# Gated mixer and attention kernel: the change of stage between the first layer and the attention, with first phases among full products, the last gelu among the first exponentials, and the first k and q loaded during the last pass

## The chip, the cores and the metric

One NeuronCore of a Trainium2 chip runs the whole program. The time is device microseconds of that core for one execution; the median of several executions counts, and one further execution was taken by the hardware profiler. Engines are named as in the profile: PE is TensorE (PEld its weight loads), ACT is ScalarE, DVE is VectorE, POOL is GpSimd, SP is SyncE, which only issues DMAs.

## The reference

The input x has 2048 tokens of 512 channels. Two branches are mixed by a gate per token.

```python
g = _sigmoid((x * gate_w).sum(-1, keepdims=True))
a = _A_ref(x, A_wqkv, A_wo)                # attention: 32 heads of 16, softmax over 2048 keys, then wo
b = _B_ref(x, B_w1, B_b1, B_w2, B_b2)      # layernorm; over tokens: w1 (2048 to 1792), gelu, w2 (1792 to 2048)
return g * a + (1 - g) * b
```

All tensors are float32. The kernel writes a float32 operand as a high and a low part and multiplies hi x hi, hi x lo and lo x hi, so that one product of the reference is three matmuls.

## The kernel before

The program is one function, gated_mix, in four stages.

1. **Values, keys, queries** (to about 139 us in the profile). x is loaded, turned and split; v stays in SBUF. k and q of all heads are computed, split into parts and stored to DRAM (kp, qp). The shift of the exponent's argument is a further 16 rows per head: in q the bound, stored in qp; in k the constant -1.
2. **First layer** (L460 to L523, to 290.9 us). The 1792 rows of u are made in four passes over f0: three of 512 rows, the last of 256. A pass has 16 steps, one for each 128 tokens; the last one goes through the second half of the tokens first, then the first half. Each step needs one block of w1: `load_weight` has SP load it (w_raw, 4 buffers), `split_weight` casts it on ACT (w_hi, 3 buffers) and subtracts on POOL (w_lo). `weight()` loads and splits ahead: in the last three steps of the last pass the blocks split are already the first ones of w2. I call these **A, B, C, D**: A holds rows 0 to 3 (of 14 blocks of u) for the first tile of outputs, B 4 to 7, C 8 to 11, D 12 and 13. When a pass is over, `gelu` (L468) takes each of its banks through add (DVE), Square (ACT), scale and multiply (DVE), Tanh (ACT), a further multiply (DVE), a cast to u_hi (ACT) and a subtraction to u_lo (DVE). The gelus of one pass run beside the next one. Those of the last pass, numbers 12 and 13, have no next pass: the loop at L521 runs them after it.
3. **Attention with the second layer beside it** (L883 on, to about 1260 us). 32 groups (16 pairs of heads, two halves of the queries) have 8 phases each, of 8 score matmuls of 64 rows. In the other 64 rows of TensorE runs half of a matmul of the second layer: a product is done in two halves in two phases (`dense`, a list by pairs of phases; L1024). Behind a phase come the value matmuls of the phase before (`apply_v`, L861). ACT takes the exponentials of the scores (L926) out of a ring of seven banks, so the eighth score of a phase waits for a bank of its own phase. In some phases DVE computes one pair of exponentials instead. Ahead of the first phase the list `first` holds 28 full products of the second layer (128 rows each, L892); 14 x 3 = 42 products make one tile of outputs.
4. **The end**: output projections, gate, stores.

k and q of a pair of heads stand stacked in tiles ks (two buffers) and qs: `load_k` (L552) brings three blocks of 16 rows for each of two heads, 128 KB each, `load_q` (L557) four of 64 KB. The rows of -1 in the two k buffers are memset: the first on POOL (L541), the second on DVE (L1039) at the end of phase 0. The k buffers lie where the first layer's second half of h lay, so the first load of k can start when the last pass has left that half.

What sets the order: inside `tc.manual_schedule(...)` the instructions of the named engines keep the order of the code (all five engines in stage 3; ACT, DVE and POOL in the first and last pass of the first layer). Two such parts, and what stands outside, are merged by the framework's scheduler by priority. Each engine then works its own queue strictly in order. Every DMA here is issued by SP, whose queue is one more such queue; a DMA also waits there for the eighth before it.

Of the kernel before, what the change touches and what calls it, by code (L numbers as in the profile page):

```python
# [76 lines left out]
def gated_mix(ctx: ExitStack, tc: tile.TileContext, a_x, a_wqkv, a_wo, b_w1, b_b1, b_w2, b_b2, gate_w, out):  # L77
# [18 lines left out]
    qp_d = [dram.tile([3, P, S], F32, name=f"qp{b}") for b in range(ND)]  # L96
    most_d = dram.tile([P, ND], F32, name="most_d")
    kp_d = [dram.tile([2, P, S], F32, name=f"kp{b}") for b in range(ND)]

# [60 lines left out]
    def weight():  # L160
        load_weight()
        split_weight()
        return ready.pop(0)
# [24 lines left out]
    with tc.tile_pool(name="vp", bufs=1, side="right") as pool:  # L188
# [74 lines left out]
        with tc.manual_schedule():  # L263
# [64 lines left out]
            for t in range(2, NS):  # L328
                if t + 1 < TURNED:
                    turn(t + 1)  # L330
                if t + 2 < NS:
                    turn_blocks(t + 2)
                row_stats(t - 2)
                if t + 5 < NS:
                    load_blocks(t + 5)
                if t + 3 < NS:
                    load(t + 3)
                if t == 4:
                    turn_biases(bias_tiles)
                if t in (6, 9):  # L340
                    qk_w.append(load_wcols(qk_cols.pop(0)))
                if t in (9, 12):
                    qk_w.append(split_wcols(*qk_w.pop(0)))
                ps = bank()
                products(ps, v_pairs(t))
                v_out(t, ps)
# [119 lines left out]
    with tc.tile_pool(name="ln1", bufs=3, side="right") as ln, tc.tile_pool(name="gl", bufs=2, side="right") as gl:  # L466

        def gelu(ps, fb):  # L468

            u = gl.tile([P, D], F32, name="gu")  # L470
            s = gl.tile([P, D], F32, name="gs")
            hi, lo = u_hi[:, fb, :], u_lo[:, fb, :]
            nc.vector.tensor_scalar_add(u, ps, b1[:, fb : fb + 1])
            yield
            nc.scalar.activation(s, u, AF.Square)
            yield
            nc.vector.tensor_scalar(s, s, GELU_A, 1.0, ALU.mult, ALU.add)
            nc.vector.tensor_mul(s, s, u)
            yield
            nc.scalar.activation(s, s, AF.Tanh, scale=GELU_C)  # L480
# [13 lines left out]
        STEPS = 7  # L494
        gelus = []
        for f0, cs in order.items():
# [37 lines left out]

    def shift_rows(engine, t):
        for i in range(2):
            engine.memset(t[i * HALF + SHIFT[0] : i * HALF + SHIFT[0] + DH].bitcast(F32), -1.0)


    with tc.issue_after(subs[-1].ins):  # L540
        shift_rows(nc.gpsimd, k_bufs[0])  # L541


    def stack(dst, src, which, pair, cols, planes):
        b, r0 = divmod(pair * 2 * DH, P)
        for i in range(2):
            rows = slice(r0 + i * DH, r0 + (i + 1) * DH)
# [3 lines left out]

    def load_k(g):  # L552
        t = k_bufs[g % 2]
        stack(t, kp_d, 1, g % NP, slice(0, S), PAIRS)
        return t

    def load_q(g):  # L557
        half, pair = divmod(g, NP)
        t = stk.tile([P, QW], F32R, name="qs")
        stack(t, qp_d, 0, pair, slice(half * QW, (half + 1) * QW), [*PAIRS, SHIFT])  # L560
        return t

    def second_out(t, ps):
        bp = out_pool.tile([P, D], F32, name="row", bufs=3)
        nc.vector.tensor_scalar(bp, ps, b2x2[:, t : t + 1], omg[:, t : t + 1], ALU.add, ALU.mult)
        nc.sync.dma_start(bp_d[t], bp)

    acc_ctx.close()

# [182 lines left out]
    steps = second_layer(0)  # L752
    first, at = steps[:28], put(steps[28:], 0, [8, 6])
    for t in range(1, NS):
# [129 lines left out]
    with tc.manual_schedule(engines=engines):  # L884
        kt, qt = {0: load_k(0)}, {0: load_q(0)}
        late, fence = None, None

        for n, (step, *args) in enumerate(first):
            if n and n % 12 == 0:
                split_weight(nc.vector.tensor_copy, nc.vector.tensor_tensor)  # L890
            ps, a, b, start, stop, done = step(*args)
            nc.tensor.matmul(ps, a, b, start=start, stop=stop)  # L892
            if done:
                done()

# [80 lines left out]
        for grp in range(NG):  # L976
            at = [0, 0]
            for ph in range(2 * TWOS):
# [237 lines left out]
```

## Time and profile before

| | |
|---|---|
| median of 3 runs | 1272.56 us (1272.41 to 1272.59) |
| profiled execution | 1272.19 us |
| its span, first to last instruction | 1270.4 us |
| TensorE busy | 1261.4 us, 99% of the span |
| ScalarE, VectorE, GpSimd busy | 84%, 57%, 18% |
| granted TensorE clock | 0.999 |
| end of the first layer, first score, first value product | 290.9, 298.0, 303.5 us |

A matmul of 512 columns shows as 0.39 us, but the next one starts 0.23 us after it, since they are pipelined; what counts is the distance of the starts. In a timeline row stand start, duration, engine, line, operation, tiles and count, and in brackets how long the engine was idle before and what ended that. A row with a count xN covers N instructions that follow each other.

### The profile page before, as it was taken

The numbers are of one execution on the slowest core, as the hardware profiler recorded it, in microseconds if no ns is written. First come the engines' busy times: TensorE is split into PE (matmuls) and PEld (weight loads), VectorE is DVE, ScalarE is ACT, GpSimd is POOL, SyncE is SP. The second block draws the span as 40 slices with busy tenths as digits, with TensorE's granted clock in tenths as the row PEclk, the third lists the DMA queues.
The fourth block names the chain that finished last, engine by engine and source line by source line (L and its number), as shares of the span: only waits on it lengthen the run. The fifth ranks groups of instructions, "written<-read, shape, count | busy, mean of one in ns | idle before, by whom it ended". The sixth has DMA issues, their size and how long they took to land.

```text
span 1270.4 us, 33041 instructions
## 1 busy us (share of the span) xinstructions
PE 1261.4 (99%) x13230; PEld 797.6 (63%) x13230; DVE 725.9 (57%) x1329; ACT 1072.8 (84%) x1484; POOL 229.4 (18%) x447
## 2 busy tenths in 40 slices
PE   9999999999999999999999999999999999999997
PEld 7888888886555555555555555555555555555555
DVE  6775371537776776666634346676666662325425
ACT  4444343438999999999999999999999999999994
POOL 4510244453111111111110011111111111100000
PEclk9999999999999999999999999999999999999999
DMA  7787633327343343334555533333334345447721
GB/s 203 209 292 290 230 111 100 98 75 160 72 93 60 76 86 70 77 67 85 114 106 118 131 64 71 68 73 76 75 72 73 76 89 103 98 87 195 151 61 70
DMA packets 101554, 140.53 MB, mean 111 GB/s; under 512 B 17081, under 2 KB 62287, under 8 KB 98320
## 3 DMA queue, kind: packets, MB, share of 16 engines
q1 hardware_dynamic: 100816, 137.29, 46.0%
q8 instruction: 106, 1.74, 0.6%
q10 hardware_dynamic: 576, 1.05, 0.2%
q14 instruction: 56, 0.46, 0.1%
HBM read 102.25 MB, written 36.03 MB: 109 GB/s over the span
## 4 chain that ended last, share of the span: by engine, by line
PE 98%; DMA 1%; ACT 0%; DVE 0%; issue 0%; SPq 0%
PE s L861 38%; PE s L903 33%; PE acc L464 12%; PE acc L91 10%; PE dn L1024 4%; PE pa L1095 1%; PE acc L298 0%; DMA ks<-kp 0%; ACT pt L926 0%; PE acc L271 0%; DMA qs<-qp 0%; PE pa L1104 0%; PE acc L209 0%; DVE base L1117 0%; SPq L149 0%
## 5 line engine op out<-in xcount | busy, mean ns | idle before, releaser
L926 ACT ACTIVATE pt<-s 128x512 f32<-128x512 f32 (+1 forms) x1259 | 943.7, 961 | 10.1 <-PE s L903 4.9
L903 PE MATMUL s<-qs,ks 64*128 64x512 f32 x2048 | 494.0, 404 | 1.4 <-DMA qs<-qp 0.6
L861 PE MATMUL s<-pt,v 128*17 128x256 f32 x8024 | 482.6, 381 | 0.0
L903 PEld LDWEIGHTS s<-qs,ks 64*128 64x128 f32 x2048 | 325.2, 184 | 168.7 <-ACT pt L926 91.2
L881 DVE TENSOR_TENSOR ot<-s,ot 128x256 f32<-128x256 f32 (+2 forms) x427 | 190.4, 447 | 348.4 <-PE s L861 272.3
L861 PEld LDWEIGHTS s<-pt,v 128*17 128x17 f32 x8024 | 210.3, 97 | 232.5 <-ACT pt L926 85.0
L1024 PE MATMUL dn<-u_hi,w_hi 64*128 64x512 f32 x428 | 186.5, 436 | 0.0
L84 POOL TENSOR_TENSOR w_lo<-w_raw,w_hi 128x512 fp32r<-128x512 f32 (+1 forms) x126 | 148.7, 1182 | 169.4 <-ACT w_hi L83 109.7
L1024 PE MATMUL dn<-u_lo,w_hi 64*128 64x512 f32 x430 | 170.1, 395 | 0.0
L1024 PE MATMUL dn<-u_hi,w_lo 64*128 64x512 f32 x430 | 169.1, 393 | 0.0
L1028 POOL MEMSET token<- 1x1 f32 x256 | 26.4, 103 | 780.0 <-PE dn L1024 659.4
L948 DVE SCALAR_TENSOR_TENSOR row<-row,o_hi 128x512 f32<-128x512 f32 x168 | 116.6, 694 | 4.9
L83 ACT CAST w_hi<-w_raw 128x512 fp32r<-128x512 f32 (+1 forms) x67 | 37.9, 569 | 80.3 <-PE acc L464 59.9
L464 PE MATMUL acc<-h_hi,w_hi 128*128 128x512 f32 x224 | 87.1, 389 | 0.0
L464 PE MATMUL acc<-h_lo,w_hi 128*128 128x512 f32 x224 | 87.1, 389 | 0.0
L464 PE MATMUL acc<-h_hi,w_lo 128*128 128x512 f32 x224 | 87.1, 389 | 0.0
L1024 PEld LDWEIGHTS dn<-u_hi,w_lo 64*128 64x128 f32 x430 | 79.3, 184 | 1.3
L1024 PEld LDWEIGHTS dn<-u_lo,w_hi 64*128 64x128 f32 x430 | 79.4, 185 | 0.5
L1024 PEld LDWEIGHTS dn<-u_hi,w_hi 64*128 64x128 f32 x428 | 78.6, 184 | 1.1
L91 PE MATMUL acc<-xt_hi,wc_hi 128*128 128x512 f32 x128 | 49.8, 389 | 0.0
L91 PE MATMUL acc<-xt_lo,wc_hi 128*128 128x512 f32 x128 | 49.8, 389 | 0.0
L91 PE MATMUL acc<-xt_hi,wc_lo 128*128 128x512 f32 x128 | 49.8, 389 | 0.0
(148 smaller groups left out, 1163.6 us busy)
## 6 DMA issues: line engine op xcount, KB each, us to landing
w_raw<-in_B_w_dram SPq DMA_DIRECT2D x96, 256.0 KB
ks<-kp SPq DMA_DIRECT2D x192, 128.0 KB
qs<-qp SPq DMA_DIRECT2D x256, 64.0 KB
qp<-pc SPq DMA_DIRECT2D x16, 768.0 KB
x<-in_A_x_dram SPq DMA_DIRECT2D x32, 256.0 KB
kp<-pc SPq DMA_DIRECT2D x16, 512.0 KB
w_raw<-in_B_w_dram SPq DMA_DIRECT2D x32, 128.0 KB
bp<-row SPq DMA_DIRECT2D x16, 256.0 KB
```

Source lines behind the costliest of these rows:

```text
L83: copy(hi, src)
L84: return sub(lo, src, hi.bitcast(F32), ALU.subtract)
L91: nc.tensor.matmul(ps, a, b, start=start and n == 0, stop=stop and n == last)
L464: nc.tensor.matmul(p, a, b, start=first and k == 0, stop=last and k == 2)
L861: mm = nc.tensor.matmul(av[32 * j : 32 * j + VC, i * QC : (i + 1) * QC], v[:, c, g % NP * 2 + i, :], pt[:, h * QC : (h + 1) * QC], start=t ...
L881: reads(nc.vector.tensor_tensor(x, y, x, ALU.add), bank)
L903: mm = nc.tensor.matmul(banks[:, bank, :], kt[grp][rows, c * P : (c + 1) * P], qt[grp][rows, qb * NB : (qb + 1) * NB], start=True, stop=True,)
L926: act = nc.scalar.activation(dst, banks[:, at[0] : at[-1] + 1, :], AF.Exp, scale=SCALE)
L948: nc.vector.scalar_tensor_tensor(box[1], q or box[1], a, x, ALU.add, ALU.mult)
L1024: mm = nc.tensor.matmul(ps, a[half], b[half], start=first and not second, stop=last and bool(second))
L1028: fence = nc.gpsimd.memset(token, 0.0)
L1095: nc.tensor.matmul(pa[t], a, b, start=i == 0 and t not in LATE, stop=i == len(mms) - 1 and t in LATE)
```

## The change

- **Order of the second layer's first tile.** `first` has the products 0 to 15; the next 8 (16 to 23) go as halves beside the scores of phases 0 and 1; a new list `between` has products 24 to 35 as full ones, put behind the scores of phase 0 and ahead of those of phase 1; the last six go with phases 2 and 3 as before.
- **Gelus 12 and 13.** Their add is issued where the loop at L521 stood, the next four steps of both ahead of `first`, and the last two (cast and subtraction) after each of the first four scores of phase 0. Since their buffers are gone by then, they take tiles of the later stage (row, ot).
- **First k and q.** `load_k` and `load_q` can load one head alone. The four loads of the first pair are issued with the priority of given steps of the last pass (the list `marks` holds the priority at each step).
- **Rows of -1.** A DRAM tensor minus_d is filled once, in the value stage (POOL memset and one store by SP at tile 5); load_k copies it into each k buffer the first time. The memsets of POOL and DVE go.
- **Splits.** Block D is split on DVE at the end of phase 0; the two splits among `first` go.

```diff
+    minus_d = dram.tile([DH, S], F32, name="minus_d")
...
+                if t == 5:
+                    minus = pool.tile([P, DH * S // P], F32, name="minus")
+                    nc.gpsimd.memset(minus, -1.0)
+                    nc.sync.dma_start(minus_d.rearrange("r (a c) -> (r a) c", a=P // DH), minus)
...
-        def gelu(ps, fb):
+        def gelu(ps, fb, places=None):
...
+            u, s = places() if places else (gl.tile([P, D], F32, name=name) for name in ("gu", "gs"))
...
+                    marks = [*marks, tc.cur_priority]
...
-            gelus = [gelu(ps[i], f0 // P + i) for i in range(n)]
-        for step in gelus:
-            list(step)
+            places = (lambda: last_places.pop(0)) if f0 + NB >= F else None
+            gelus = [gelu(ps[i], f0 // P + i, places) for i in range(n)]
...
-    with tc.issue_after(subs[-1].ins):
-        shift_rows(nc.gpsimd, k_bufs[0])
...
+        if g < 2:
+            for i in heads:
+                at = i * HALF + SHIFT[0]
+                nc.sync.dma_start(t[at : at + DH].bitcast(F32), minus_d)
...
+    q_first, marks = None, marks[-NH:]
+    for i in range(2):
+        with tc.high_priority(offset=tc.cur_priority - marks[i * NH // 2]):
+            load_k(0, [i])
+        with tc.high_priority(offset=tc.cur_priority - marks[i * NH // 2 + 2]):
+            q_first = load_q(0, q_first, [i])
...
+    for step in gelus:
+        next(step)
     acc_ctx.close()
...
-    first, at = steps[:28], put(steps[28:], 0, [8, 6])
+    first, between, at = steps[:16], steps[24:36], put(steps[16:24] + steps[36:], 0, [8, 6])
...
-        kt, qt = {0: load_k(0)}, {0: load_q(0)}
+        kt, qt = {0: k_bufs[0]}, {0: q_first}
...
+        for _ in range(4):
+            for step in gelus:
+                next(step)
+        full(first)
...
+                    if grp == ph == 0 and m < 4:
+                        next(gelus[m % 2])
...
                 if grp == ph == 0:
-                    shift_rows(nc.vector, k_bufs[1])
+                    split_weight(nc.vector.tensor_copy, nc.vector.tensor_tensor)
+                    full(between)
```

ScalarE's queue at the change of stage, before. L83 casts a weight block: w_hi_2613 is the last block of w1, w_hi_2627 is A, w_hi_2641 B, w_hi_2654 C. gu_2548 and gu_2564 belong to gelus 10 and 11, gu_2665 and gu_2675 to 12 and 13; L475 is Square, L480 Tanh, L484 the cast to u_hi.

```order
L83 CAST w_hi_2613<-w_raw_2597 128x256
L484 CAST u_hi_1405<-gu_2548 128x512
L83 CAST w_hi_2627<-w_raw_2611 128x512
L484 CAST u_hi_1405<-gu_2564 128x512
L83 CAST w_hi_2641<-w_raw_2625 128x512
L475 ACTIVATE gs_2666<-gu_2665 128x512
L83 CAST w_hi_2654<-w_raw_2639 128x512
L475 ACTIVATE gs_2676<-gu_2675 128x512
L480 ACTIVATE gs_2666<-gs_2666 128x512
L480 ACTIVATE gs_2676<-gs_2676 128x512
L484 CAST u_hi_1405<-gu_2665 128x512
L484 CAST u_hi_1405<-gu_2675 128x512
```

The exponentials follow, all after these. The same place in the changed kernel, from behind the cast of gelu 10: w_hi_2631 is A, w_hi_2645 B, w_hi_2658 C; row_2718 and ot_2719 belong to gelu 12, row_2720 and row_2721 to gelu 13; L479 is Square, L484 now Tanh, L488 the cast to u_hi, L938 an exponential.

```order
L479 ACTIVATE ot_2719<-row_2718 128x512
L479 ACTIVATE row_2721<-row_2720 128x512
L83 CAST w_hi_2631<-w_raw_2615 128x512
L488 CAST u_hi_1409<-gu_2568 128x512
L484 ACTIVATE ot_2719<-ot_2719 128x512
L484 ACTIVATE row_2721<-row_2721 128x512
L83 CAST w_hi_2645<-w_raw_2629 128x512
L83 CAST w_hi_2658<-w_raw_2643 128x512
L938 ACTIVATE pt_2823<-s_2777 128x512
L488 CAST u_hi_1409<-row_2718 128x512
L938 ACTIVATE pt_2823<-s_2777 128x512
L488 CAST u_hi_1409<-row_2720 128x512
```

Both Squares have moved ahead of A, both Tanhs ahead of B and C, and the casts of gelus 12 and 13 behind the first and the second exponential.

SP's queue, before, from the first load of k on: w_raw_2582 and w_raw_2597 are the last pass's 15th and 16th block, then A, B, C, D.

```order
L550 DMA ks0_2715<-kp0_65 16x2048
L149 DMA w_raw_2582<-in_B_w1_dram 128x256
L149 DMA w_raw_2597<-in_B_w1_dram 128x256
L149 DMA w_raw_2611<-in_B_w2_dram 128x4x128
L149 DMA w_raw_2625<-in_B_w2_dram 128x4x128
L550 DMA ks0_2715<-kp0_65 16x2048
L149 DMA w_raw_2639<-in_B_w2_dram 128x4x128
L149 DMA w_raw_2652<-in_B_w2_dram 128x2x128
L550 DMA ks0_2715<-kp0_65 16x2048 x4
L550 DMA qs_2781<-qp0_60 16x1024 x8
```

The same place after, where w_raw_2586 and w_raw_2601 are the 15th and 16th block, w_raw_2615 is A and w_raw_2629 B; C follows behind the last row, then three loads of q, then D.

```order
L545 DMA ks0_2699<-kp0_66 16x2048 x3
L553 DMA ks0_2699<-minus_d_65 16x2048
L545 DMA qs_2705<-qp0_60 16x1024
L150 DMA w_raw_2586<-in_B_w1_dram 128x256
L545 DMA qs_2705<-qp0_60 16x1024 x3
L150 DMA w_raw_2601<-in_B_w1_dram 128x256
L545 DMA ks0_2699<-kp0_66 16x2048
L150 DMA w_raw_2615<-in_B_w2_dram 128x4x128
L545 DMA ks0_2699<-kp0_66 16x2048 x2
L553 DMA ks0_2699<-minus_d_65 16x2048
L150 DMA w_raw_2629<-in_B_w2_dram 128x4x128
L545 DMA qs_2705<-qp0_60 16x1024
```

The first head's k, its rows of -1 and its q have moved ahead of the last two blocks of w1, and the second head's k ahead of and between A and B.

More of the change, by code (lines that the diff above doesn't have):

```diff
@@ L466, in gated_mix @@
     with tc.tile_pool(name="ln1", bufs=3, side="right") as ln, tc.tile_pool(name="gl", bufs=2, side="right") as gl:
-        def gelu(ps, fb):
-            u = gl.tile([P, D], F32, name="gu")
-            s = gl.tile([P, D], F32, name="gs")
+        def gelu(ps, fb, places=None):
+            u, s = places() if places else (gl.tile([P, D], F32, name=name) for name in ("gu", "gs"))
             hi, lo = u_hi[:, fb, :], u_lo[:, fb, :]
@@ L494, in gated_mix @@
         STEPS = 7
-        gelus = []
+        gelus, marks = [], []
         for f0, cs in order.items():
@@ L533, in gated_mix, with stack @@
     k_bufs = [stk.tile([P, S], F32R, name=f"ks{i}", bufs=1) for i in range(2)]
-    def shift_rows(engine, t):
-        for i in range(2):
-            engine.memset(t[i * HALF + SHIFT[0] : i * HALF + SHIFT[0] + DH].bitcast(F32), -1.0)
-    with tc.issue_after(subs[-1].ins):
-        shift_rows(nc.gpsimd, k_bufs[0])
-    def stack(dst, src, which, pair, cols, planes):
+    def stack(dst, src, which, pair, cols, planes, heads):
         b, r0 = divmod(pair * 2 * DH, P)
-        for i in range(2):
+        for i in heads:
             rows = slice(r0 + i * DH, r0 + (i + 1) * DH)
@@ L550, in stack, with load_k, load_q @@
                 nc.sync.dma_start(dst[at].bitcast(F32), src[b][part[which], rows, cols])
-    def load_k(g):
+    def load_k(g, heads=range(2)):
         t = k_bufs[g % 2]
-        stack(t, kp_d, 1, g % NP, slice(0, S), PAIRS)
+        stack(t, kp_d, 1, g % NP, slice(0, S), PAIRS, heads)
+        if g < 2:
+            for i in heads:
+                at = i * HALF + SHIFT[0]
+                nc.sync.dma_start(t[at : at + DH].bitcast(F32), minus_d)
         return t
-    def load_q(g):
+    def load_q(g, t=None, heads=range(2)):
         half, pair = divmod(g, NP)
-        t = stk.tile([P, QW], F32R, name="qs")
-        stack(t, qp_d, 0, pair, slice(half * QW, (half + 1) * QW), [*PAIRS, SHIFT])
-        return t
+        if t is None:
+            t = stk.tile([P, QW], F32R, name="qs")
+        stack(t, qp_d, 0, pair, slice(half * QW, (half + 1) * QW), [*PAIRS, SHIFT], heads)
+        return t
+    q_first, marks = None, marks[-NH:]
[4 more added lines that the diff above has]
+            q_first = load_q(0, q_first, [i])
     def second_out(t, ps):
@@ L566, in second_out @@
         nc.sync.dma_start(bp_d[t], bp)
+    last_places = [[out_pool.tile([P, D], F32, name=n, bufs=b) for n, b in x] for x in ((("row", 3), ("ot", 2)), (("row", 3),) * 2)]
+    for step in gelus:
+        next(step)
     acc_ctx.close()
@@ L884, in gated_mix, with full @@
     with tc.manual_schedule(engines=engines):
-        kt, qt = {0: load_k(0)}, {0: load_q(0)}
+        kt, qt = {0: k_bufs[0]}, {0: q_first}
         late, fence = None, None
[L888 to L894, printed above, removed]
+        def full(steps):
+            for step, *args in steps:
+                ps, a, b, start, stop, _ = step(*args)
+                nc.tensor.matmul(ps, a, b, start=start, stop=stop)
+        for _ in range(4):
+            for step in gelus:
+                next(step)
+        full(first)
         pt = None
```

## The prediction, made before the changed kernel ran

> **What bounds the kernel now.** The page comes first: who is busy, and which work forms the chain that ended last.
>
> ```profile
> PE 1261.4 (99%) x13230; PEld 797.6 (63%) x13230; DVE 725.9 (57%) x1329; ACT 1072.8 (84%) x1484; POOL 229.4 (18%) x447
> PE 98%; DMA 1%; ACT 0%; DVE 0%; issue 0%; SPq 0%
> ```
>
> TensorE is the bound nearly everywhere, so an edit that neither adds nor removes products can only move time where TensorE stands still. The chain, cut to the change of stage, shows where that is (columns: start, us, what).
>
> ```profile
> 288.56 6.21 DMA ks<-kp
> 294.79 3.24 DMA qs<-qp
> 298.03 0.47 PE s L903
> 298.53 1.65 ACT pt L926 x3
> 300.40 1.97 ACT pt L926 x2
> 302.37 0.04 issue
> 302.42 0.50 PE s L903
> ```
>
> From 298 to 303.6 the chain runs through the first q load and the first exponentials. TensorE's own timeline gives the size.
>
> ```profile
> 290.67 0.39 PE L464 MATMUL acc<-h_hi,w_lo 128*128 128x512 f32 x1
> 290.90 0.39 PE L892 MATMUL dn<-u_hi,w_hi 128*128 128x512 f32 x1
> ...
> 297.02 0.39 PE L892 MATMUL dn<-u_hi,w_hi 128*128 128x512 f32 x1
> 298.02 0.46 PE L903 MATMUL s<-qs,ks 64*128 64x512 f32 x1 [0.62 <-DMA qs<-qp]
> ...
> 300.63 0.46 PE L903 MATMUL s<-qs,ks 64*128 64x512 f32 x1 [0.50 <-POOL token L1028]
> ...
> 302.42 0.50 PE L903 MATMUL s<-qs,ks 64*128 64x512 f32 x1 [0.18 <-ACT pt L926]
> ...
> 303.54 1.92 PE L861 MATMUL s<-pt,v 128*17 128x256 f32 x32
> 305.40 0.50 PE L903 MATMUL s<-qs,ks 64*128 64x512 f32 x1
> ...
> 307.23 1.06 PE L861 MATMUL s<-pt,v 128*17 128x256 f32 x16
> ```
>
> The 28 full products start 0.227 us apart ((297.02 - 290.90) / 27) and take 6.35 us. A phase of eight scores with eight half products takes 307.23 - 305.40 = 1.83 us when nothing holds it. From 290.90 to the first value products at 303.54 are 12.64 us; the work in them is 6.35 + 2 x 1.83 = 10.01. So **TensorE stands still for 2.6 us** here, and that is all the change can win: 0.2% of the kernel, about what a measurement of it can tell from no change, and the bound that I use for "same".
>
> **The change, part by part.** The products are the same before and after (16 full, 16 halves, 12 full instead of 28 and 16), so the sum is: standstill after, less 2.6.
>
> *Loads of k and q.* They go out from 280.34 instead of mostly from 288.56, so q no longer ends a wait. The 2.6 go as far as nothing else is late.
>
> *The last two gelus.* The order in the section on the change shows ScalarE's queue: Square of gelus 12 and 13 now stand ahead of the cast of weight block A, and the Tanhs ahead of B and C. Each engine works its queue in order. The rows of before for these instructions:
>
> ```profile
> 288.19 0.62 ACT L83 CAST w_hi<-w_raw 128x512 fp32r<-128x512 f32 x1 [0.43 <-POOL w_lo L84]
> ...
> 292.59 0.62 ACT L83 CAST w_hi<-w_raw 128x512 fp32r<-128x512 f32 x1 [0.53 <-DMA w_raw<-in_B_w_dram]
> 293.12 0.63 ACT L475 ACTIVATE gs<-gu 128x512 f32<-128x512 f32 x1
> 293.65 0.61 ACT L480 ACTIVATE gs<-gs 128x512 f32<-128x512 f32 x1
> ```
>
> ```profile
> 225.23 0.43 DVE L477 TENSOR_SCALAR gs<-gs 128x512 f32<-128x512 f32 x1
> ...
> 290.66 1.40 DVE L473 TENSOR_SCALAR gu<-acc,b 128x512 f32<-128x512 f32 x2
> ...
> 292.79 0.69 DVE L478 TENSOR_TENSOR gs<-gs,gu 128x512 f32<-128x512 f32 x1
> 293.78 1.14 DVE L477 TENSOR_SCALAR gs<-gs 128x512 f32<-128x512 f32 x1 [0.30 <-ACT gs L475]
> ```
>
> ```profile
> 288.89 1.30 POOL L84 TENSOR_TENSOR w_lo<-w_raw,w_hi 128x512 fp32r<-128x512 f32 x1 [0.78 <-ACT w_hi L83]
> ...
> 293.29 1.34 POOL L84 TENSOR_TENSOR w_lo<-w_raw,w_hi 128x512 fp32r<-128x512 f32 x1 [0.82 <-ACT w_hi L83]
> ```
>
> Before, A was cast at 288.19, while the last pass still ran. After, step by step, with 0.04 for a hand-over (the chain's "issue" at 302.37):
> - The last first-layer product ends at 290.67 + 0.39 = 291.06. VectorE's add for gelu 13 takes 0.74: 291.84. Square 13 starts at 291.87; the next ScalarE instruction starts 0.53 later (292.59 to 293.12, 293.12 to 293.65), so A's cast runs from 292.40 to 293.02. The first full product starts at 293.08, not 290.90: **+2.18**.
> - A's low part is GpSimd's, 0.08 behind the cast (288.81 to 288.89) and 1.30 long: 294.40. The third product, ready at 293.53, starts at 294.45: **+0.92**.
> - B's cast waits for Tanh 13. VectorE: scale 12 in 0.43 and multiply 12 in 0.69, to 293.03; scale 13 then meets GpSimd's A. At 293.78 such a scale took 1.14 and ended 0.29 behind GpSimd's row (293.29 + 1.34 = 294.63), against 0.43 undisturbed; so it ends at 294.69, multiply 13 at 295.38, Tanh starts at 295.42, B's cast at 295.95, to 296.57. GpSimd makes its low part by 297.95. The 15th product, due at 297.17, starts at 298.00: **+0.83**.
> - The first score starts at 298.00 + 2 x 0.227 = 298.45; it was 298.02. The earlier scores are not earlier.
> - Two casts of u stand between the first exponentials, 0.53 each. Phase 0's exponentials took 298.53 to 302.37 = 3.84; now 4.90, from 298.95 to 303.85. TensorE meanwhile has phase 0 (to 300.28) and the 12 full products (2.72, to 303.00), and the score that needs the last of them is the fifth, at 303.92: no standstill. Without these 12 products the casts would cost 1.06.
>
> Standstill after: 2.18 + 0.92 + 0.83 = 3.93. **Sum: 3.93 - 2.61 = +1.3 us.** After 303.54 TensorE never waited, and ScalarE is as far behind it as before, so the shift stays to the end.
>
> On the pair that meet at 293.1: VectorE's scale 13 could start at 293.07, GpSimd at 293.10. The Trainium skill, SBUF — State Buffer, section "Who interferes with whom", says that the two share one port pair as an exclusive lock, and whoever starts first holds it for its whole instruction. The 1.14 against 0.43 agrees. By that rule VectorE might get both of its steps in first; A's low part would then come about 1.1 later and B's factor earlier, and I estimate the sum at +1.6.
>
> *What the moved loads meet.* SP's queue and the transfers around the change of stage:
>
> ```profile
> 280.34 0.55 SPq L550 DMA_DIRECT2D ks<-kp  x1
> 281.29 4.94 SPq L149 DMA_DIRECT2D w_raw<-in_B_w_dram  x4
> ...
> 290.45 6.57 SPq L550 DMA_DIRECT2D qs<-qp  x8
> ```
>
> ```profile
> 280.30:286.80 6.50, 6.50 (x30) 5.39 (x29) 5.65 (x9) 3.90 (x9) 4.75 (x6) 1.00 0.44 123
> 286.80:298.80 12.00, 11.38 (x53) 9.21 (x53) 10.61 (x15) 7.11 (x13) 8.72 (x7) 1.00 0.88 162
> ```
>
> The second row is full (0.88 of the engines, 162 GB/s); the first has room. Four k or minus rows and one q now stand ahead of the last pass's 15th block, three q more ahead of its 16th. Estimated at 162 GB/s from 281.7 on (1.4 behind the first issue, my choice), the 15th (704 KB in all) has landed at 286.1 and the 16th (1024 KB in all) at 288.2. TensorE needs the 16th's low part at 289.99:
>
> ```profile
> 286.83 0.41 ACT L83 CAST w_hi<-w_raw 128x256 fp32r<-128x256 f32 x1 [0.42 <-issue]
> ...
> 287.32 0.80 POOL L84 TENSOR_TENSOR w_lo<-w_raw,w_hi 128x256 fp32r<-128x256 f32 x1 [0.35 <-ACT w_hi L83]
> ...
> 289.99 0.39 PE L464 MATMUL acc<-h_hi,w_lo 128*128 128x512 f32 x1
> ```
>
> A cast of 0.41 and a low part of 0.80 behind a landing at 288.2 end at 289.5, half a us in time. The least is nothing. The most: block C, in the full stretch, was issued at 287.00 at the earliest and waited for until 292.59, 5.6 us; with that, and an issue at 284.2, the 16th would land at 289.8 and TensorE stand 1.1 more, or 1.7 with the 15th late too. I take nothing, being nearer to the rows of the lighter stretch. B and C (2048 and 2368 KB, at 294.7 and 296.7) come before ScalarE wants them (295.95, 298.3); were they a us late, the sum would grow by as much.
>
> *minus_d.* No row writes it. One 128 KB store and a GpSimd fill go into the value stage.
>
> ```profile
> 24.00 1.79 POOL L84 TENSOR_TENSOR xt_lo<-xw,xt_hi 128x512 fp32r<-128x512 f32 x1 [0.75 <-ACT xt_hi L83]
> ...
> 25.99 1.85 SPq L225 DMA_DIRECT2D xb<-in_A_x_dram  x4
> ...
> 31.76 1.09 DVE L230 STREAM_TRANSPOSE xw<-xb 128x512 f32<-128x512 f32 x1
> ```
>
> The store waits for the fill behind GpSimd's row that ends at 25.79, so the x blocks due at 25.99 go out about 0.5 late and, behind 128 KB more, land about 1.2 late; VectorE turns them at 31.76, 3.9 us after the last was issued. Nothing, at most 0.3. VectorE also loses two fills of k, 3.5 us on an engine that TensorE did not wait for there: nothing.
>
> **Rivals.** *The bubble closes (faster).* If A were cast before the pass ends, the 2.6 would go and nothing come: 1270.0. For it: q and k are there. Against it: A's cast stands behind Square 13, which reads the bank that the last product writes. 3%.
> *The moved loads hold up the last pass (slower).* One mechanism: SP issues the last w1 blocks behind k and q, at the price above, up to 1.7 on top of 1.3. Past 1.25 more it is slower by 0.2%: 1275.2 to 1275.6. For it: half a us of cover by my estimate. Against it: the 16th cast ended 2.3 us ahead of its first product (287.24 to 289.54). 16%.
> *The clock falls in the wait (slower).* TensorE stands 2.2 us at one place. Its granted clock stayed 1.00 through the stops of before; only the last stretch shows less:
>
> ```profile
> 1260.00:1270.40 10.40, 4.04 (x18) 2.97 (x16) 3.75 (x5) 0.00 (x0) 0.00 (x0) 0.93 0.53 191
> ```
>
> There TensorE worked 4.04 of 10.40 us. If half clock followed for 3.4 us, 1.7 more: 1275.6. 4%. The Trainium skill, TensorE: Matmul & The Clock Gate, section "What's actually happening", gives an idle window of about 3.4 us for the fall to half clock; the wait here is shorter, so by that rule no fall comes.
>
> **Numbers.** The profiled execution took 1272.19 (span 1270.4), the median of the runs is 1272.56: plus 1.3 is 1273.5 and 1273.9. I say 1273.9. Low end: B in time (-0.83) and a little besides, 1272.8. High end: last pass late by 1.7 with a little from B or C, 1276.2. Forecast 77%, all of it within 0.2% (1270.0 to 1275.1); faster 3%, slower 16 + 4 = 20%.
>
> **What would show it.** Right: TensorE idle from 291 to 293.1 before the first full product, released by ScalarE's cast of w_hi; a second stop of 0.9 behind GpSimd's w_lo; the first score near 298.4; no wait for DMA there; value products near 304.9. Wrong: full products straight at 290.9, or gaps among the first-layer products after 287, which would put the cost in the loads.

## The result, and the profile after

The changed kernel takes **1277.95 us** (median of 6 runs, 1276.65 to 1279.8). The kernel before takes 1272.49 beside it. The ratio is 1.0044, 95% interval 1.0034 to 1.0055: slower by 0.44%, where I forecast no measurable change (1273.9, range to 1276.2). The profiled execution took 1276.65, the quickest of the six, with a span of 1274.9; the profile of before has 1270.4.

The page of the changed kernel hardly shows it: its first table and its chain by engine read almost as before.

```profile
PE 1264.1 (99%) x13230; PEld 797.2 (63%) x13230; DVE 720.1 (56%) x1326; ACT 1072.5 (84%) x1484; POOL 227.7 (18%) x447
PE 98%; DMA 1%; DVE 0%; POOL 0%; SPq 0%; issue 0%; ACT 0%; ACTq 0%
```

The chain in order of time, cut to the change of stage, shows what replaced the q load and the exponentials (columns: start, us, what):

```profile
281.18 3.90 DMA ks<-kp
...
285.14 4.92 DMA w_raw<-in_B_w_dram
...
290.15 0.42 ACT w_hi L83
...
290.64 0.75 POOL w_lo L84
...
291.97 1.45 DVE row L477 x2
...
293.98 0.61 ACT w_hi L83
...
294.66 1.40 POOL w_lo L84
...
296.10 4.48 PE dn L901 x14
```

Read it downwards. A row of k lands at 285.08, and only then does SP issue the last pass's 16th block. That block lands at 290.06 and its low part is done at 291.39, so the last products of the first layer come late. Then come VectorE's adds for the moved gelus, the second Square, A's cast and A's low part. TensorE's timeline of the same stretch:

```profile
292.23 0.39 PE L469 MATMUL acc<-h_hi,w_lo 128*128 128x512 f32 x1
294.63 0.61 PE L901 MATMUL dn<-u_hi,w_hi 128*128 128x512 f32 x1 [2.01 <-ACT w_hi L83]
295.04 0.63 PE L901 MATMUL dn<-u_lo,w_hi 128*128 128x512 f32 x1
296.10 0.80 PE L901 MATMUL dn<-u_hi,w_lo 128*128 128x512 f32 x1 [0.43 <-POOL w_lo L84]
296.69 0.63 PE L901 MATMUL dn<-u_hi,w_hi 128*128 128x512 f32 x1
297.12 0.63 PE L901 MATMUL dn<-u_lo,w_hi 128*128 128x512 f32 x1
...
300.19 0.39 PE L901 MATMUL dn<-u_hi,w_hi 128*128 128x512 f32 x1
300.51 0.49 PE L915 MATMUL s<-qs,ks 64*128 64x512 f32 x1
...
300.84 0.39 PE L915 MATMUL s<-qs,ks 64*128 64x512 f32 x1
...
302.24 0.39 PE L915 MATMUL s<-qs,ks 64*128 64x512 f32 x1
...
302.56 0.50 PE L901 MATMUL dn<-u_hi,w_hi 128*128 128x512 f32 x1
...
307.55 1.71 PE L871 MATMUL s<-pt,v 128*17 128x256 f32 x28
```

The last first-layer product starts at 292.23, against 290.67 before. The first full product follows 2.40 later instead of 0.23. Products then stand 0.43 apart (296.69 to 297.12) instead of 0.23: TensorE runs at half clock. The value products start at 307.55 instead of 303.54. Both bets that I had put at 16% and 4% came in, and in the same execution. The granted clock, in four stretches of 3.41 us, the third of which is the one at half clock (columns after the stretch: its length, busy us of PE, PEld, DVE, ACT and POOL with the number of instructions, then the clock, the share of the DMA engines, GB/s):

```profile
288.05:291.46 3.41, 3.25 (x13) 1.52 (x11) 1.14 (x2) 1.87 (x4) 1.56 (x3) 1.00 1.37 216
291.46:294.87 3.41, 1.40 (x5) 0.88 (x6) 3.33 (x6) 2.06 (x4) 0.59 (x2) 1.00 0.90 94
294.87:298.28 3.41, 2.98 (x7) 1.86 (x7) 3.38 (x5) 2.21 (x5) 1.61 (x2) 0.50 1.17 208
298.28:301.69 3.41, 3.41 (x20) 2.52 (x21) 0.12 (x1) 0.97 (x3) 2.52 (x2) 1.00 0.76 176
```

A stretch of 3.41 us in which TensorE is busy for 1.40 is followed by one of 3.41 at half clock.

So that each run can be read in the same way, the table cuts every profile at four places: the first product of the first layer (138.58 in before), its last product (290.67), the first value product (303.54), the last one (1252.83). It gives, in us, by how much each piece is longer than in the profile of before, with "rest" for what lies behind. The profiled times and medians stand beside it; the medians of before in the three groups of runs were 1271.97 to 1272.15.

| run | start | first layer | change of stage | attention | rest | profiled | median |
|---|---|---|---|---|---|---|---|
| changed | 0.40 | 1.16 | 2.44 | 0.35 | 0.11 | 1276.65 | 1277.95 |
| e5 changed, again | 0.82 | 1.56 | 4.26 | 0.47 | 0.17 | 1279.47 | 1278.22 |
| e1 loads late | 0.74 | 0.00 | 4.75 | 0.49 | 0.66 | 1278.83 | 1278.53 |
| e2 A first | 2.51 | 1.45 | 2.14 | 0.28 | -0.08 | 1278.49 | 1276.76 |
| e3 wait filled | 0.13 | 1.40 | 2.24 | 0.33 | 0.03 | 1276.39 | 1276.55 |
| e4 loads only | 0.04 | 1.59 | 4.83 | -0.11 | 0.00 | 1278.53 | 1279.12 |
| e6 rows of -1 filled | 0.57 | 0.04 | 2.69 | 2.61 | 0.14 | 1278.34 | 1278.74 |
| e7 reordered | 0.58 | 0.00 | -0.72 | 2.71 | 0.00 | 1274.85 | 1274.92 |
| e8 C ahead | 0.31 | 0.00 | 0.57 | 2.61 | -0.14 | 1275.63 | 1275.79 |
| e9 k1 loaded | 0.62 | 0.00 | -0.74 | 0.29 | 0.10 | 1272.47 | 1273.02 |
| e10 fill later | 0.69 | 0.00 | -0.96 | 0.26 | 0.10 | 1272.38 | 1272.38 |
| e11 loads reordered alone | 0.23 | 0.00 | 0.77 | -0.12 | 0.15 | 1273.22 | 1274.25 |
| e12 before, again | 0.58 | 0.00 | -0.59 | -0.05 | 0.16 | 1272.38 | - |

### The profile page after: what moved, and what is told of

It reads as the page before. It is cut to its first block, busy times and chain, and to the rows that moved or that the text cites. A ratio compares the mean times of both kernels' runs of the same rounds, so it can differ in the third digit from the quotient of the medians.

```text
span 1274.9 us, 33040 instructions
## 1 busy us (share of the span) xinstructions
PE 1264.1 (99%) x13230; PEld 797.2 (63%) x13230; DVE 720.1 (56%) x1326; ACT 1072.5 (84%) x1484; POOL 227.7 (18%) x447
## 4 chain that ended last, share of the span: by engine, by line
PE 98%; DMA 1%; DVE 0%; POOL 0%; SPq 0%; issue 0%; ACT 0%; ACTq 0%
PE s L871 38%; PE s L915 34%; PE acc L469 11%; PE acc L91 10%; PE dn L1038 3%; PE pa L1110 1%; PE dn L901 1%; PE acc L299 0%; DMA w_raw<-in_B_w_dram 0%; DMA x<-in_A_x_dram 0%; DMA ks<-kp 0%; PE pa L1119 0%; POOL w_lo L84 0%; PE acc L210 0%; DVE row L477 0%
## 5 line engine op out<-in xcount | busy, mean ns | idle before, releaser
L938 ACT ACTIVATE pt<-s 128x512 f32<-128x512 f32 (+1 forms) x1259 | 943.9, 961 | 12.9 <-PE s L915 6.9
L83 ACT CAST w_hi<-w_raw 128x512 fp32r<-128x512 f32 (+1 forms) x67 | 37.9, 569 | 81.3 <-PE acc L469 58.3
```

The source lines that it names most:

```text
L83: copy(hi, src)
L938: act = nc.scalar.activation(dst, banks[:, at[0] : at[-1] + 1, :], AF.Exp, scale=SCALE)
```

## The experiments

My theory from the trace of after was one cause with three effects: the loads of k and q, put ahead of the last blocks of w1 and w2, make the last pass late, make A late and so leave its cast behind the Squares in ScalarE's queue, and the thin stretch this leaves on TensorE brings half clock. The rivals: the moved gelus and products themselves cost the time, or the half clock was chance.

**e1: the loads back at their old place.**

```diff
-        with tc.high_priority(offset=tc.cur_priority - marks[i * NH // 2]):
-            load_k(0, [i])
-        with tc.high_priority(offset=tc.cur_priority - marks[i * NH // 2 + 2]):
-            q_first = load_q(0, q_first, [i])
+    load_k(0)
+    q_first = load_q(0)
```

> The changed kernel with the first k and q loaded at their old place in SP's queue, behind blocks A to D; all else as changed. My theory (late w1 blocks behind k and q hold up the last pass by 1.15 us; they also make A's cast stand behind the Squares; the thin stretch that follows brings half clock): the first-layer products run without a gap, the first full product follows at once, and the price moves to q, which lands near 299.5: TensorE stands some 5 us from 294.6 on, the clock falls to one half for about 3.4 us behind it, and the time is about 1277.5. Rival 1 (the half clock has nothing to do with standing still): the clock stays at 1.00, 1275.8. Rival 2 (the last pass is held up by the gelus and casts, not by the loads): the gaps of 1.15 us at 288.6 to 291.5 stay.

1278.53 (1277.88 to 1278.83, ratio 1.0048, 1.0031 to 1.0065). The first layer is 0.00 late, as the theory had it and rival 2 did not; A and B are cast ahead of the Squares again. TensorE waits for q instead:

```profile
300.10 0.76 PE L911 MATMUL s<-qs,ks 64*128 64x512 f32 x1 [4.68 <-DMA qs<-qp]
```

The clock fell in this wait too, against rival 1, for 6.8 us and not 3.4, from 297.42 on. That, the start 0.74 late and 0.66 behind the last value product (not looked into) can account for the us above the 1277.5 expected. So the moved products need the early loads: with 16 instead of 28 of them ahead of the first score, q is 4.7 late.

**e2: A's cast ahead of the Squares.**

```diff
...
-            nc.scalar.activation(s, u, AF.Square)
+            with tc.issue_after(w_casts[-3].ins) if places else ExitStack():
+                nc.scalar.activation(s, u, AF.Square)
```

> The changed kernel with the cast of block A put ahead of the two Squares in ScalarE's queue; the loads stay early. My theory: the queue is only part of the wait, A itself lands at about 292.1; its cast starts near 292.2 instead of 293.98 and the first full product near 292.9, 1.8 earlier. The third waits for A's low part until about 294.3, and B, which lands at 296.3, then holds the 13th to 15th product: first score near 298.9 instead of 300.5. The stretch is less thin, so the clock may stay at 1.00. About 1276.3, 1.6 less than the changed kernel. Rival (the Squares in front are the whole of the wait, as the prediction had it): the first full product follows the last first-layer product at once, and the time falls by over 2.4, below 1275.5. The last pass stays 1.15 late by either.

1276.76 (1276.29 to 1278.49, ratio 1.0034, 1.0020 to 1.0049). TensorE's waits at the change of stage:

```profile
295.40 0.50 PE L905 MATMUL dn<-u_hi,w_hi 128*128 128x512 f32 x1 [0.38 <-ACT w_hi L85]
...
296.76 0.50 PE L905 MATMUL dn<-u_hi,w_lo 128*128 128x512 f32 x1 [0.63 <-POOL w_lo L86]
...
300.61 0.50 PE L905 MATMUL dn<-u_hi,w_hi 128*128 128x512 f32 x1 [1.27 <-ACT w_hi L85]
...
301.96 0.50 PE L905 MATMUL dn<-u_hi,w_lo 128*128 128x512 f32 x1 [0.62 <-POOL w_lo L86]
```

The first wait shrinks from 2.01 to 0.38, the 0.38 being A's own landing. But B, behind both Tanhs, now costs 1.27 and 0.62 ten products later. The change of stage gains 0.3, although the clock stayed at 1.00 there. (All of this profile is 2.5 late from its start; see the last section.) My theory had the first wait nearly right and B's price too low: the first score came 0.3 earlier against the end of the pass, not 1.6. One wait was exchanged for another; that the total came near the 1276.3 expected was luck, as far as this profile shows. The rival falls.

**e3: nine products, of no use, in the wait for A.**

```diff
-        full(first)
...
+        for _ in range(9):
+            nc.tensor.matmul(ps, u_hi[:, 0, :P], u_hi[:, 0, :], start=True, stop=True)
...
```

> The changed kernel with nine extra products (u_hi by u_hi, into the bank that the first full product then overwrites; they add nothing to the output) issued on TensorE in the wait for A, 2.04 us of work. My theory: the half clock comes from the thin stretch, so the granted clock stays at 1.00 from 291 to 305. The full products then run 0.227 apart, but B's low part, done near 299.3, holds the 15th, so that the first score comes near 299.8 instead of 300.5: 0.7 less than the changed kernel, about 1277.2. Rival 1: the clock falls all the same, and the time stays at 1278 or above. Rival 2 (a clock fall is worth its full 1.7 us): 1276.2.

1276.55 (1276.09 to 1277.13, ratio 1.0036, 1.0023 to 1.0048). The clock stayed at 1.00 throughout, against rival 1. What was left:

```profile
296.06 0.50 PE L901 MATMUL dn<-u_hi,w_lo 128*128 128x512 f32 x1 [0.71 <-POOL w_lo L84]
...
299.55 0.50 PE L901 MATMUL dn<-u_hi,w_lo 128*128 128x512 f32 x1 [0.43 <-POOL w_lo L84]
```

A's and B's low parts hold TensorE for 1.14, so only 0.2 of the change of stage is gained over the changed kernel's profile. The first score came at 300.22, not at 299.8. The median is 1.4 below the changed kernel's (ratios 1.0036 and 1.0044), with intervals that overlap, and lies between the 1277.2 of my theory and the 1276.2 of rival 2, so it does not decide between them. What makes up the rest of the 1.4 is not shown.

**e4: of the change the early loads alone.**

```diff
-    first, between, at = steps[:16], steps[24:36], put(steps[16:24] + steps[36:], 0, [8, 6])
+    first, at = steps[:28], put(steps[28:], 0, [8, 6])
...
-        next(step)
+        list(step)
```

> The changed kernel with the last two gelus and the full products as before the change (gelus whole behind the last pass, 28 full products ahead of the first phase, none between): of the change only the early loads and the rows of -1 from DRAM are left. My theory (the early loads do the harm, by late w1 blocks, a late A and the clock): the last pass is 1.15 late, A's cast still stands behind the Squares, the first full product waits some 2 us and the clock falls; the first two phases then wait for their exponentials as they did before: 1279 to 1280, no better than the changed kernel. Rival (the harm is in the moved gelus and products): the time falls to 1274 or below.

1279.12 (1278.53 to 1279.78, ratio 1.0056, 1.0039 to 1.0073). First layer 1.59 late, the first wait for A again 2.01, half clock again for 3.4 us, all without the moved gelus and products. A's cast, at 294.05, stands behind both Squares (292.82 and 293.51) here too. The rival falls.

**e5: the changed kernel again.** No edit.

> The changed kernel unaltered, to see what repeats. My theory (late blocks, then a wait, then half clock, each caused by the one before): the same picture, with the 15th and 16th block released by their loads, the last pass 1.1 to 1.2 us late, a first wait of about 2.0 us for A and half clock for about 3.4 us behind it; 1277 to 1279. Rival (the half clock was chance): the clock stays at 1.00 in this stage and the time is near 1276.

1278.22 (1277.52 to 1279.47, ratio 1.0044, 1.0028 to 1.0061). All of it repeats, with a longer half clock:

```profile
292.78:296.19 3.41, 1.39 (x5) 0.49 (x3) 3.34 (x6) 2.56 (x5) 0.71 (x1) 1.00 0.97 134
296.19:299.60 3.41, 2.69 (x6) 2.18 (x7) 3.02 (x4) 2.02 (x4) 1.61 (x2) 0.50 1.17 190
299.60:303.01 3.41, 3.41 (x9) 2.34 (x7) 0.00 (x0) 0.00 (x0) 1.97 (x2) 0.50 0.64 173
```

Two stretches at 0.50 instead of one make this execution's change of stage 1.82 longer than that of the first profile (4.26 against 2.44). It is not what puts the first median 1.3 above the first profile: the two runs at that median, 1277.92 and 1277.99, have a granted clock of 0.998 on record, the profiled one 0.997, while a second such stretch would take 0.0013 more off (1.7 of 1275 us). What made those runs longer stays open.

**e6: the rows of -1 filled instead of loaded.**

```diff
...
-        if g < 2:
-            for i in heads:
-                at = i * HALF + SHIFT[0]
-                nc.sync.dma_start(t[at : at + DH].bitcast(F32), minus_d)
...
+    for i, n in enumerate((-4, -2)):
+        with tc.issue_after(subs[n].ins):
+            shift_rows(nc.gpsimd, k_bufs[0], i)
...
+                if grp == 0 and ph in (2, 3):
+                    shift_rows(nc.vector, k_bufs[1], ph - 2)
```

> The changed kernel with the rows of -1 filled by GpSimd and VectorE again instead of loaded from DRAM: two loads of 128 KB fewer in SP's queue, one of them ahead of the 15th and 16th block; A's cast now stands between the two Squares. My theory (a k row takes about 1.0 us of the queue, and the blocks wait for those ahead of them): the 15th and the 16th land 1.0 earlier, the last pass is 0.4 late instead of 1.15, A's cast comes half a us earlier against the pass's end, B lands about 2 us earlier, near 294.3, and the time falls by some 1.2 to 1.7, to about 1276.5. Rival (the rows of -1 travel beside the others and cost nothing): no change in the last pass, 1277.5 to 1278.

1278.74 (1278.34 to 1280.39, ratio 1.0055, 1.0038 to 1.0071): no gain in time, where I expected 1.2 to 1.7, but the first layer is 0.04 late instead of 1.16. Taking one row of 128 KB from ahead of the 15th block took away that whole delay. The gain was lost in "attention", 2.3 more than in the changed kernel: my own fills of the second k buffer. A's wait (1.31) and half clock stayed.

**e7 and e8: k and q behind the 16th block.** Both have e6's fills; e8 uses (6, 6) for the first pair.

```diff
-    for i in range(2):
+    for i, (mk, mq) in enumerate(((5, 5), (7, 7))):
-        with tc.high_priority(offset=tc.cur_priority - marks[i * NH // 2]):
+        with tc.high_priority(offset=tc.cur_priority - marks[mk]):
             load_k(0, [i])
-        with tc.high_priority(offset=tc.cur_priority - marks[i * NH // 2 + 2]):
+        with tc.high_priority(offset=tc.cur_priority - marks[mq]):
```

> The changed kernel with rows of -1 filled by GpSimd, and with the first k and q in SP's queue behind the 16th block and A: the first head's k and q around B, the second head's around and behind C. The casts of A and B then stand ahead of the Squares. My theory (the harm of the change lies in the place of these loads alone): the last pass runs through, the first full product follows it at once at 290.9, the 16 full products end near 294.6, k and q of the first head have landed by about 294, and TensorE stands still only for exponentials that come behind the second Tanh: value products near 302.6 instead of 303.5, so 1271.5 to 1272.5, level with the kernel before or a little less. Rival 1 (k and q come late here too): TensorE stands 1 to 2 us for q at 294.6, 1273 to 1274. Rival 2 (the moved gelus and products themselves cost): above 1275.

> As the one before, but with the first head's k and q around and behind C, so that the casts of A, B and C all stand ahead of the Squares. My theory: the last pass runs through here too, the Squares and Tanhs come about 1.2 later than in the one before, the exponentials stand behind the second Tanh, near 296.6, and the value products near 303.1: 1272 to 1273. Rival (ScalarE's order no longer matters once the blocks are in time): the same time as the one before.

e7: 1274.92 (1274.45 to 1275.55, ratio 1.0021, 1.0012 to 1.0031); e8: 1275.79 (1275.38 to 1276.53, ratio 1.0027, 1.0016 to 1.0038). Both miss their totals. In both the first layer is 0.00 late, there is no wait for A or B, and the clock stays at 1.00. e7 bears out the stage: its change of stage is 0.72 shorter than before. e8 does not: 0.57 longer, where I expected 0.4 shorter. It waits for q and for exponentials that come behind later Tanhs, so ScalarE's order still matters and its rival falls:

```profile
295.93 0.46 PE L913 MATMUL s<-qs,ks 64*128 64x512 f32 x1 [0.75 <-DMA qs<-qp]
...
298.99 0.50 PE L913 MATMUL s<-qs,ks 64*128 64x512 f32 x1 [1.19 <-ACT pt L936]
```

e7's two waits of TensorE from 286 to 312:

```profile
297.96 0.50 PE L913 MATMUL s<-qs,ks 64*128 64x512 f32 x1 [0.69 <-ACT pt L936]
...
311.27 0.50 PE L913 MATMUL s<-qs,ks 64*128 64x512 f32 x2 [1.09 <-DVE ot L889]
```

The second of e7's is the fill again, on VectorE ahead of the addition that empties a bank:

```profile
308.99 1.76 DVE L535 MEMSET ks<- 16x2048 f32 x1 [0.48 <-PE s L913]
310.79 0.42 DVE L889 TENSOR_TENSOR ot<-s,ot 128x256 f32<-128x256 f32 x1
```

**e9 and e10: without VectorE's fills.** The second k buffer's rows of -1 are loaded; e10 has GpSimd's second fill behind C's low part as well.

```diff
-        if g < 2:
+        if g == 1:
...
-    for i, n in enumerate((-4, -2)):
+    for i, n in enumerate((-4, -1)):
```

> e7 again, with the rows of -1 of the second k buffer loaded from DRAM, as the changed kernel does, instead of filled by VectorE in phases 2 and 3; in the profile of e7 those fills stood between a score and the bank it waited for, 1.1 us once and 2.5 us in all. My theory (e7's gain of 0.72 at the change of stage was hidden by these fills): the stage stays 0.7 shorter than before, the 2.4 us later on go, and the time is 1272.0 to 1272.6, level with the kernel before. Rival (the 2.5 us of e7 come from the new order of phases): it stays at 1274.9.

> As e9, with GpSimd's second fill of the first k buffer moved from behind B's low part to behind C's, so that VectorE's scale of gelu 13 (1.39 us beside the fill in e7, 0.43 alone) no longer runs beside it. My theory: the second Tanh comes 0.9 earlier and with it the exponentials; value products 0.5 to 0.9 earlier than in e9: 1271.3 to 1272.0, the best of all. Rival (the second fill is then itself late for the first score of the second head): no gain over e9, or 0.5 lost.

e9: 1273.02 (1271.6 to 1275.79, ratio 1.0008, 0.9999 to 1.0017); e10: 1272.38 (1271.3 to 1276.0, ratio 1.0009, 0.9999 to 1.0018). "Attention" is back at 0.29 and 0.26, and the change of stage is 0.74 and 0.96 shorter than before. So the 2.5 us were the fills', and e9's rival falls. Both medians lie some 0.4 above what I expected, and e10's value products come 0.22 earlier than e9's, not 0.5 to 0.9. Both are level with the kernel before: no version that beats it was found.

**e11: the harmless loads alone.** e10's loads and fills with the first pair (6, 6), and e4's gelus and products.

> The early loads in the harmless place, with C ahead of the Squares, and nothing else of the change: gelus whole behind the last pass, 28 full products, none between; rows of -1 as in e10. My theory: 28 products run from 290.9 to 297.3, q is there, the first score comes 0.7 earlier than before, and the two waits for exponentials of before (0.50 and 0.18) stay or grow: 0.3 to 0.7 less than before at the change of stage, 1271.4 to 1272.2. Rival (C, now landing behind k and q rows, is late for the 25th product): TensorE waits there 0.5 to 1.5, 1272 to 1273.5.

1274.25 (1273.22 to 1275.53, ratio 1.0017, 1.0008 to 1.0027): a miss for both. C is in time and the first score 0.5 early, but TensorE then waits for exponentials:

```profile
300.19 0.50 PE L923 MATMUL s<-qs,ks 64*128 64x512 f32 x1 [0.55 <-ACT pt L946]
...
301.64 0.47 PE L923 MATMUL s<-qs,ks 64*128 64x512 f32 x1 [0.95 <-ACT pt L946]
...
303.42 0.49 PE L923 MATMUL s<-qs,ks 64*128 64x512 f32 x1 [0.18 <-ACT pt L946]
```

Against e10, which differs by the moved gelus and products and by where k, q and C's load stand, the change of stage is 1.7 longer. But the place of these loads alone made 1.29 between e7 and e8, and against e8, which has them where e11 has them (and GpSimd's second fill earlier), e11 is only 0.20 longer. How much the moved gelus and products gain by themselves, once the blocks are in time, is therefore not shown.

**e12: the kernel before, a second profile.**

> The kernel before once more, for a second profile: the changed kernels' first products came 0.04 to 2.5 us late in the first 7 us, ahead of anything that was edited. My theory (this is the spread of the start, no matter which kernel): the start differs from the first profile by some tenths here too, and all else is the same within 0.2. Rival (the start is slower because of the edit): the same start as in the first profile.

1272.38. Its first layer starts 0.58 late, and its first score comes at the same 298.02: most of k and all of q went out 0.58 later too (from 289.14 instead of 288.56), but the q that ends the wait landed at the same time.

## Why the prediction was wrong, point by point

The difference between the profiles is 4.46 us of span: 0.40 + 1.16 + 2.44 + 0.35 + 0.11. I forecast 1.3, all of it in the third piece.

1. **The moved loads and the last pass: this step failed.** I wrote "half a us in time" and "I take nothing, being nearer to the rows of the lighter stretch". I had the 15th block landing at 286.1 and the 16th at 288.2; the 16th landed at 290.06, and TensorE was 1.16 late. My end of 1.1, with a landing at 289.8, came near the truth, in part by luck: the 16th went out 0.94 later than the 284.2 that I had there and took 4.92 instead of 5.6, and the 15th, cast only at 288.18, was late as well. My sum ran the bytes ahead of the 16th block, 1024 KB, at 162 GB/s from 281.7 on. The rate was right, the bytes were not; the stretch up to the landing, as a row:

```profile
281.70:290.06 8.36, 8.28 (x37) 6.30 (x36) 5.09 (x7) 3.76 (x8) 3.69 (x4) 1.00 1.07 159
```

8.36 us at 159 GB/s are 1300 KB: blocks still under way from before and loads issued behind the 16th took part of the rate. And the chain shows SP not issuing the 16th until a k row has landed, which a sum over bytes leaves out. e6 shows how near the edge it was: one row fewer, and the delay is gone. That the early k and q, put ahead of the blocks, were the cause is shown by e1 and e7 to e11, all at 0.00, and by e4, late with these loads alone.

2. **A's cast and the first full product: right in size.** Forecast 2.18 behind the pass, measured 2.40 - 0.23 = 2.17, released by ScalarE's w_hi. But two things were other than I wrote. I put the order of ScalarE's queue down to the moved gelus; e4, with the gelus unmoved, has A's cast behind both Squares, and e1, with the gelus moved and the loads late, has it ahead, so it was the loads' doing. And the queue was not all: SP issued A only at 287.13, and its own landing was late too, as e2 shows with 0.38.

3. **The low parts: right in kind, somewhat high.** Forecast 0.92 for A's and 0.83 for B's. At full clock (e3) they cost 0.71 and 0.43. In the changed kernel B's is not seen, since half clock slowed the products in front of it.

4. **The clock: this step failed too.** I priced it at 1.7 and gave it 4%, because "its granted clock stayed 1.00 through the stops of before". Those stops took less out of a stretch: in the emptier of the two that hold them, from 299.65 to 303.06, TensorE was still busy for 2.59 of 3.41. In the first profile half clock cost less than 1.7, since part of its time would have gone into B's stop: the 16 full products took 300.51 - 294.63 = 5.88, forecast 298.45 - 293.08 = 5.37, and 300.22 - 294.62 = 5.60 in e3 at full clock. So it cost 0.3 to 0.5 there, and 1.8 more in e5.

5. **From the first score to the value products: mis-sized by 0.64.** Forecast 304.85 - 298.45 = 6.40, measured 307.55 - 300.51 = 7.04. No wait is in it. I read the 1.83 off the wrong phase: the one at 305.40 in before has six half products, not eight, and its last two scores run side by side,

```profile
306.90 0.40 PE L903 MATMUL s<-qs,ks 64*128 64x512 f32 x2
```

so it holds seven starts. A phase with eight takes 302.56 - 300.51 = 2.05, which makes 0.43 for the two. The other 0.2 is in the 12 full products, 305.51 - 302.56 = 2.95 instead of 2.72: where full products and halves meet, neighbours stand 0.32 to 0.34 apart (300.19 to 300.51, 300.51 to 300.84, 302.24 to 302.56) instead of 0.23, and the changed order has more such places. With 2.05 a phase, the standstill of before was 12.64 - 6.35 - 4.10 = 2.2 and not 2.6.

6. **The start: 0.40 that I did not have.** It arises in the first 7 us, ahead of any edit. e12 lost 0.58 there and had it back at the change of stage (-0.59): q landed at the same time although it was sent for later, and the wait for q was so much shorter. One run does not show whether that is more than chance; in the changed kernel no wait for q is left that could shrink.

7. **The store of the rows of -1: right at nothing.** From 8 us to the last pass no product shifts further.

8. **Attention, 0.35: open.** It is 0.26 to 0.49 in the runs with the moved products and without VectorE's fills, and -0.12 to -0.05 with the old order, so it belongs to that order. In the changed kernel most of it comes in three steps far behind the change of stage, between 500 and 530 us (0.09), 770 and 800 (0.12) and 1010 and 1040 (0.21). By what mechanism was not found.

On the port pair, the rule of the Trainium skill, SBUF — State Buffer, section "Who interferes with whom", agrees: the multiply of gelu 13 took 1.65 (from 294.94) beside A's low part (from 294.66), against 0.69. My working had put the meeting on the scale, which took 0.42. The rivals' worst fault was that I weighed them as alternatives. The late blocks thinned the stretch behind which the clock fell, so they came together, and the range had room for one.

## What to carry to other kernels

Before a transfer is moved ahead in a queue, list what then stands behind it and when each of those is needed; the price is theirs, and half a microsecond of estimated cover is none. A load that ends a wait may also be hiding other delays, which appear once it is early. Where two risks feed each other, their prices add up in the range. And a price per phase is read off a phase that has the same work in it.

## What the runs showed of the hardware that I had not expected

**Half clock does not need a long standstill.** The longest single stop of the changed kernel was 2.0 us. What the falls at the change of stage had in common is the busy share of the stretch of 3.41 us in front. It was low there (1.40, 1.39, in e1 1.41 and in e4 1.31 of 3.41), and the highest that brought a fall was e6's:

```profile
290.81:294.22 3.41, 1.61 (x6) 0.67 (x4) 3.32 (x5) 2.19 (x4) 3.19 (x3) 1.00 1.00 138
```

The lowest that brought none was in e2:

```profile
298.27:301.68 3.41, 1.79 (x7) 0.85 (x5) 2.37 (x5) 2.29 (x4) 1.05 (x1) 1.00 1.13 212
```

So the line lay between 0.47 and 0.53 of TensorE's busy time here. Where the products end, near 1265 us, stretches counted on in the same steps fit it: 0.35 to 1.42 us busy brought the fall in seven runs, 1.85 in before and 2.14 in e5 did not. At half clock the share that freed the clock was 0.87 in the changed kernel (2.98 of 3.41), while 0.79 in e5 (2.69) did not, which made the difference of 1.8 us between these two executions. The Trainium skill, TensorE: Matmul & The Clock Gate, section "What's actually happening", tells of a free-running window of 3413 ns; the falls of 3.41 and 6.83 us agree. It asks for an idle window; here windows that were up to 0.47 busy sufficed, and the measurement decides.

**A start can fall to half clock too.** The 2.5 us of e2's start lie there, behind a wait of 0.94 for a load of x:

```profile
4.70:8.12 3.42, 2.17 (x9) 0.99 (x8) 1.99 (x3) 1.35 (x3) 0.00 (x0) 1.00 0.96 312
8.12:11.53 3.41, 3.41 (x12) 2.71 (x11) 1.89 (x3) 1.62 (x3) 0.00 (x0) 0.50 0.83 225
```

TensorE was busy for 0.63 of the stretch in front, more than elsewhere sufficed to keep the clock; so at the start the line is not where the other rows put it, and why stays open. (In e1 a first stretch with 2.24 of 3.41, 0.66, brought no fall.) Single runs of 1274 to 1276 in e9 and e10 may hold such a fall somewhere: e10's four above 1275 have granted clocks of 0.997 (three) and 0.998 on record, its other seven 0.998 or 0.999, and a stretch at half clock takes 0.0013 off. None of them was profiled, so this is not shown.
